# Half masks, transposes in two PSUM banks, and the output ahead of the state's sum, in a fused retention and MLP kernel

## Chip, cores, metric

One core of one Trainium2 chip. The metric is device time in microseconds (us), the median of a kernel's runs. PE is the tensor engine, DVE the vector engine, ACT the scalar engine, POOL GpSimd.

## The reference

Retention over q, k, v of shape (8, 8, 576, 64), followed by a dense layer, a Mish activation and a second dense layer. Cut to what matters:

```python
scores = (q @ k.T) / sqrt(64)
ret    = (scores * Dmat) @ v               # Dmat: gamma_h ** (i - j) for i >= j, else 0
x      = ret as 4608 tokens x 512
h      = x @ w_in                          # 512 x 2048
out    = (h * tanh(log1p(exp(h)))) @ w_out # 2048 x 512
```

## The kernel before

The sequence is cut into chunks of 128 positions; two chunks (same place, neighbouring batches) are a pair, four chunks a token block. For each chunk: P casts q and k to bf16 and scales them on DVE, T transposes them on PE and copies them out of PSUM, S makes the scores and masks them on DVE, O adds the product with v and the product with the running state of earlier chunks; the result, xT, feeds the dense layers. The state is summed per pair. Chunks 0 to 3 go through a start-up of their own with warming matmuls, chunks 4 to 7 are woven between blocks of the first dense layer, later ones go by pairs. Each engine gets its work in the order of the program text.

```python
def step_t(n):                       # transposes of chunk n, ACT and DVE copy them out
    tp = ps_sc.tile([P, 4, NP, P], BF16, name="sc")[:, 0:2]
    ...                              # PE: 4 transposes of q into tp[:, 0], 4 of k into tp[:, 1]
    for i, copy in enumerate((nc.scalar.copy, nc.vector.tensor_copy)):
        copy(r["qk"][:, i, u], tp[:, i])

def pair_o(m):                       # output of a pair
    sc = pairs[m][1][0]
    ot = sc.rearrange("p e (g u) i -> p e g u i", g=2)      # e: one PSUM bank each
    step_k(m)                        # PE: state products; DVE: their sum; cast to bf16
    ...                              # PE: within, across
    nc.vector.tensor_copy(xt[...], sc...)

# chunk 4 between the dense blocks i of token block 0
elif i == 8:  step_k(0)
elif i == 9:  step_n(1)              # DVE: two multiplications
elif i == 10: one(4, "P")
elif i == 12: one(4, "T")
elif i == 13: one(4, "S")
...
```

A PSUM tile of the pool `ps_sc` is 4 KB per partition. It is counted here as two banks: of its four parts (the first index of `tp`), 0 and 1 lie in one bank, 2 and 3 in the other. `[:, 0:2]` takes parts 0 and 1, `[:, ::2]` parts 0 and 2.

## Time and profile before

314.31 us (three runs).

| engine | busy us of 312.8 |
|---|---|
| PE | 300.0 |
| ACT | 136.0 |
| DVE | 123.4 |
| POOL | 78.6 |

PE is the bound. Here is pair 5's output, in order of time (start, length, engine, line, instruction, and in brackets the idle time before it and what ended it):

```profile
84.36 1.22 DVE L392 CAST xT<-sc 128x1024 bf16<-128x1024 f32 x1 [0.33 <-PE sc L361]
85.50 0.68 DVE L261 TENSOR_TENSOR qks<-qraw,gq 128x512 bf16<-128x512 f32 x1
85.64 1.90 PE L404 MATMUL hp<-xT,w_in_t 128*128 128x512 bf16 x8 [0.36 <-DVE xT L392]
```

PE stands 0.36 us for the copy that makes xT; DVE goes on with the next pair's casts at once.

### The profile page before, as it was taken

To read this page: it belongs to the slowest core of one execution; us is meant where nothing else is said; L and a number is where in the kernel's file an instruction comes from. 1 tells how busy PE (TensorE), PEld (TensorE's weight loads), DVE (VectorE), ACT (ScalarE), POOL (GpSimd) and SP (SyncE) were. 2 spreads that over 40 slices of the span, in tenths; PEclk is the share of its full clock that TensorE was granted. 3 is DMA by queue.
4 is the path that set the end of the run, shared out by engine and by line. 5 is a ranking of instruction groups with operands and counts; after the bars stand their busy time and mean duration, and the time that the engine had idled before them with its cause. 6 is when DMAs were issued, how large, how long until landed. Compare 5 with 4: busy or idle time off the path is not lost.

```text
span 312.8 us, 6059 instructions
## 1 busy us (share of the span) xinstructions
PE 300.0 (96%) x2601; PEld 157.2 (50%) x2637; DVE 123.4 (39%) x170; ACT 136.0 (43%) x237; POOL 78.6 (25%) x102
## 2 busy tenths in 40 slices
PE   6899989999999999999999999999999999999995
PEld 2355578655455545454545454545454544444444
DVE  3546465219768561626252526252525221000000
ACT  6665655422364633343434343434343433334311
POOL 6576573453340404040404040600000000000000
PEclk9999999999999999999999999999999999999999
DMA  6999999999998696959696959692313100000132
GB/s 180 255 186 226 198 207 226 201 232 248 214 230 103 132 174 141 168 137 169 142 165 143 160 144 159 138 160 63 90 47 88 48 34 36 34 34 36 40 81 80
DMA packets 71946, 43.38 MB, mean 139 GB/s; under 512 B 55664, under 2 KB 63088, under 8 KB 71920
## 3 DMA queue, kind: packets, MB, share of 16 engines
q0 software_dynamic: 43424, 26.22, 55.8%
q1 hardware_dynamic: 28352, 16.65, 20.6%
q8 instruction: 20, 0.33, 0.5%
q10 hardware_dynamic: 144, 0.13, 0.1%
q14 instruction: 6, 0.05, 0.0%
HBM read 36.70 MB, written 9.44 MB: 148 GB/s over the span
## 4 chain that ended last, share of the span: by engine, by line
PE 89%; ACT 4%; DVE 3%; issue 2%; DMA 1%; SPq 1%; ACTq 0%; DVEq 0%
PE hp L439 39%; PE hp L404 32%; PE hp L427 4%; PE sc L306 3%; PE sc L347 3%; ACT res L459 2%; PE sc L361 2%; DMA kraw<-in_k_dram 1%; PE sc L280 1%; PE hp L329 1%; PE hp L451 1%; DVE sm L309 1%; PE hp L415 1%; PE sc L329 1%; ACT qkT L282 1%
## 5 line engine op out<-in xcount | busy, mean ns | idle before, releaser
L439 PE MATMUL hp<-w_out_t,gT 128*128 128x512 bf16 x541 | 125.2, 379 | 1.2 <-issue 0.3
L404 PE MATMUL hp<-xT,w_in_t 128*128 128x512 bf16 x480 | 112.7, 379 | 1.3 <-DVE xT L392 0.4
L406 ACT ACTIVATE gT<-hp 128x512 bf16<-128x512 f32 x124 | 74.0, 597 | 36.6 <-PE hp L404 34.0
L439 PEld LDWEIGHTS <-gT 128*128 128x128 bf16 x560 | 53.3, 98 | 62.6
L404 PEld LDWEIGHTS <-w_in_t 128*128 128x128 bf16 x496 | 47.5, 97 | 57.1 <-DVE xT L392 0.9
L459 ACT COPY res<-hp 128x512 f32<-128x512 f32 x35 | 20.5, 585 | 98.4 <-PE hp L439 98.4
L309 DVE TENSOR_TENSOR sm<-sc,mask 128x1024 bf16<-128x1024 f32 x36 | 42.7, 1217 | 10.0 <-PE sc L306 10.0
L592 POOL COPY seen<-qkT 1x1 bf16<-1x1 bf16 x10 | 1.8, 176 | 121.9 <-DMA qkT<-qks 121.9
L336 DVE TENSOR_TENSOR st<-st,hp 128x512 f32<-128x512 f32 x8 | 5.5, 686 | 54.9 <-PE hp L329 54.9
L392 DVE CAST xT<-sc 128x1024 bf16<-128x1024 f32 x14 | 17.1, 1221 | 22.6 <-PE sc L361 22.2
L261 DVE TENSOR_TENSOR qks<-kraw,gk 128x512 bf16<-128x512 f32 x32 | 21.8, 683 | 1.7 <-DMA kraw<-in_k_dram 1.7
L261 DVE TENSOR_TENSOR qks<-qraw,gq 128x512 bf16<-128x512 f32 x32 | 21.8, 681 | 0.0
L112 POOL DMA_DIRECT2D qraw<-in_q_dram x16 | 17.2, 1075 | 13.9 <-DVE qks L261 9.1
L112 POOL DMA_DIRECT2D kraw<-in_k_dram x16 | 17.1, 1072 | 9.3 <-DVE ssb L338 3.7
L112 POOL DMA_DIRECT2D v<-in_v_dram x16 | 17.2, 1080 | 6.6 <-DMA kraw<-in_k_dram 2.5
L454 DVE COPY half<-hp 128x256 f32<-128x256 f32 x1 | 0.4, 425 | 43.8 <-PE hp L451 43.8
L427 PE MATMUL hp<-xT,w_in_t 128*128 128x128 bf16 x272 | 17.0, 219 | 0.0
L427 PEld LDWEIGHTS <-w_in_t 128*128 128x128 bf16 x272 | 15.5, 98 | 0.9 <-issue 0.2
L282 DVE COPY qkT<-sc 128x512 bf16<-128x512 bf16 x12 | 5.1, 422 | 23.4 <-ACT qkT L282 23.4
L429 ACT ACTIVATE gT<-hp 128x512 bf16<-128x512 f32 x17 | 10.1, 597 | 8.6 <-PE hp L427 8.6
L338 ACT CAST ssb<-st 128x512 bf16<-128x512 f32 x12 | 7.4, 618 | 14.3 <-DVE st L336 13.3
L306 PE MATMUL sc<-qkT 64*128 64x128 bf16 x288 | 11.9, 218 | 1.7 <-DVE qkT L282 1.5
(67 smaller groups left out, 163.6 us busy)
## 6 DMA issues: line engine op xcount, KB each, us to landing
out_dram<-res SPq DMA_DIRECT2D x31, 256.0 KB, 2.1
qraw<-in_q_dram POOLq DMA_DIRECT2D x12, 512.0 KB, 6.9
kraw<-in_k_dram POOLq DMA_DIRECT2D x12, 512.0 KB, 8.2
v<-in_v_dram POOLq DMA_DIRECT2D x12, 256.0 KB, 8.8
qraw<-in_q_dram POOLq DMA_DIRECT2D x8, 256.0 KB, 10.3
kraw<-in_k_dram POOLq DMA_DIRECT2D x8, 256.0 KB, 10.3
w_out_t<-in_moe_w_out_dram POOLq DMA_DIRECT2D x4, 512.0 KB, 11.7
qraw<-in_q_dram SPq DMA_DIRECT2D x8, 128.0 KB, 3.8
```

The costliest lines, as they stand in the source:

```text
L112: nc.gpsimd.dma_start(out=r[x][ds(off, ni)].rearrange("p u h d -> p (u h) d"), in_=src[ds(b, 2), :, ds(i0, ni), :].rearrange("b h p d -> p ...
L261: nc.vector.tensor_tensor(by_slots(r["qks"][:, i, u]), r[x][:, u].rearrange("p (r s) d -> p r s d", r=2), g[:, place(2 * m), :].rearrange( ...
L306: nc.tensor.matmul(sc[:, e, p, :], lhsT=qk[r, 1, u, p, :], rhs=qk[r, 0, u, p, :], start=True, stop=True)
L309: nc.vector.tensor_tensor(sm.rearrange("p e n i -> p (e n) i"), sc.rearrange("p e n i -> p (e n) i"), mask1.rearrange("p e n i -> p (e n) ...
L347: nc.tensor.matmul(ot[ds(64 * c, 64), e, g, :], lhsT=vs[:, h, :], rhs=sm[:, e, p, :], start=(start and g == 0), stop=True, skip_group_chec ...
L392: nc.vector.tensor_copy(xt[:, :, ds(s * P, 2 * P)].rearrange("p n (u i) -> p n u i", u=2), sc.rearrange("p e (g u) i -> p (e g) u i", g=2))
L404: nc.tensor.matmul(hp, lhsT=w_in_t[:, c, ts(f, P)], rhs=xts[t][:, c, :], start=(c == 0), stop=(c == KC - 1))
L406: nc.scalar.activation(gts[t][:, f, :], hp, AX.Mish)
L427: nc.tensor.matmul(hp[:, j, :], lhsT=w_in_t[:, c, ts(4 * fb + j, P)], rhs=xts[t][:, c, ts(s, P)], start=(c == 0), stop=(c == KC - 1))
L429: nc.scalar.activation(gts[t][:, ds(4 * fb, 4), ts(s, P)], hp, AX.Mish)
L439: nc.tensor.matmul(ops, lhsT=gts[t][:, f, ts(s, P)], rhs=w_out_t[:, f, :], start=(f == 0), stop=(f == nF - 1))
L459: copy(ot, ops)
```

## The change

Its intent is to shorten four waits of PE. The first two masks are done in halves, one per bank, with the next key cast between them. The two transposes of a chunk are put in two banks, so that ACT and DVE may copy at once. T and S of chunks 4 to 7 come one dense block earlier. In pair_o the output copy comes ahead of the state's sum, and for pair 5 it is shared by ACT and DVE. Cut to its core:

```diff
-        tp = ps_sc.tile([P, 4, NP, P], BF16, name="sc")[:, 0:2]
+        tp = ps_sc.tile([P, 4, NP, P], BF16, name="sc")[:, ::2]
 # step_s, chunks 0 and 1
+            for e in range(2):
+                nc.vector.tensor_tensor(sm[:, e], sc[:, e], mask1[:, e], op=OP.mult)
+                if e == 0:
+                    between()                 # the key cast of the next chunk
 # the state's cast to bf16
-        (nc.vector.tensor_copy if m < 4 else nc.scalar.copy)(ssb, st_sum[b])
+        (nc.vector.tensor_copy if b < 4 and i0 < 2 * P else nc.scalar.copy)(ssb, st_sum[b])
 # pair_o
-        step_k(m)
+        state = step_k(m)
 ...
+        if m == 5:
+            nc.scalar.copy(xv[:, 0], ot[:, 0])
+            nc.vector.tensor_copy(xv[:, 1], ot[:, 1])
+        else:
+            nc.vector.tensor_copy(...)
+        if state:
+            step_sum(*state)
 # chunk 4
         elif i == 9:
             step_n(1)
-        elif i == 10:
             one(4, "P")
-        elif i == 12:
+        elif i == 11:
             one(4, "T")
 # chunks 5 to 7: T at fb 0 (was 1), S at fb 1 (was 2), P ahead of the state
```

More of the change, by code (lines that the diff above doesn't have):

```diff
@@ L296, in step_n, with step_s @@
                 op=OP.mult)
-    def step_s(n):
+    def step_s(n, between=None):
         m, u = divmod(n, 2)
@@ L308, in step_s @@
         sm = tr.tile([P, 2, NP, P], BF16, name="sm")
-        nc.vector.tensor_tensor(
-            sm.rearrange("p e n i -> p (e n) i"), sc.rearrange("p e n i -> p (e n) i"),
-            mask1.rearrange("p e n i -> p (e n) i") if n < NCH else
-            (mask if len(chunks[n]) == 1 else mask2).unsqueeze(1).to_broadcast([P, 2 * NP, P]), op=OP.mult)
+        if between:
+            for e in range(2):
[3 more added lines that the diff above has]
+        else:
+            nc.vector.tensor_tensor(
+                sm.rearrange("p e n i -> p (e n) i"), sc.rearrange("p e n i -> p (e n) i"),
+                mask1.rearrange("p e n i -> p (e n) i") if n < NCH else
+                (mask if len(chunks[n]) == 1 else mask2).unsqueeze(1).to_broadcast([P, 2 * NP, P]), op=OP.mult)
         pairs[m][u] = (sc, sm)
@@ L317, in step_k @@
         if m >= n_pairs or len(chunks[2 * m]) > 1:
-            return
+            return None
         b, i0, _ = chunks[2 * m][0]
@@ L331, in step_k, with step_sum @@
                                      start=(u == 0 and p == 0), stop=True, skip_group_check=True)
+        return b, i0, st
+    def step_sum(b, i0, st):
         if i0 == 0:
@@ L391, in pair_o @@
         xt, s = x_of(2 * m)
-        nc.vector.tensor_copy(xt[:, :, ds(s * P, 2 * P)].rearrange("p n (u i) -> p n u i", u=2),
-                              sc.rearrange("p e (g u) i -> p (e g) u i", g=2))
+        xv = xt[:, :, ds(s * P, 2 * P)].rearrange("p (e g) (u i) -> p e g u i", e=2, u=2)
+        if m == 5:
+            nc.scalar.copy(xv[:, 0], ot[:, 0])
+            nc.vector.tensor_copy(xv[:, 1], ot[:, 1])
+        else:
+            nc.vector.tensor_copy(xv.rearrange("p e g u i -> p (e g) u i"), ot.rearrange("p e g u i -> p (e g) u i"))
+        if state:
+            step_sum(*state)
     gts = {}
@@ L487 @@
     keep_warm(3)
-    first(0, "VS")
-    first(1, "Qk")
+    first(0, "V")
+    step_s(0, lambda: first(1, "k"))
+    first(1, "Q")
     keep_warm(3)
@@ L499 @@
     keep_warm(3)
-    first(1, "S")
-    first(2, "Qk")
+    step_s(1, lambda: first(2, "k"))
+    first(2, "Q")
     keep_warm(3)
@@ L536 @@
         elif i == 8:
-            step_k(0)
+            step_sum(*step_k(0))
         elif i == 9:
             step_n(1)
-        elif i == 10:
             one(4, "P")
-        elif i == 12:
+        elif i == 11:
             one(4, "T")
@@ L555 @@
             if n < 7:
-                if fb == 1:
+                if fb == 0:
                     one(n + 1, "T")
-                elif fb == 2:
+                elif fb == 1:
                     one(n + 1, "S")
-                    if n % 2 == 0:
-                        step_k(n // 2)
                     if n < 6:
                         one(n + 2, "P")
+                    if n % 2 == 0:
+                        step_sum(*step_k(n // 2))
                 elif fb == 3:
@@ L578, in visit @@
             if m == 5:
-                step_k(1)
+                step_sum(*step_k(1))
             one(n, "T")
```

## The prediction

> **What bounds the kernel now.** I read the page's shares first, then the waits of the tensor engine (PE) by window, then the order of time in the two windows where those waits lie, then the landing times of the loads.
>
> ```profile
> PE 300.0 (96%) x2601; PEld 157.2 (50%) x2637; DVE 123.4 (39%) x170; ACT 136.0 (43%) x237; POOL 78.6 (25%) x102
> ```
>
> PE is busy for 300.0 of 312.8 us, so a change that touches no matmul can only take idle PE time, about 12.8 us. Of that, some 3.5 us lie behind the last matmul (305.80 + 3.51 = 309.3 in the chain of work that ended last, against a span of 312.8), and the change leaves the tail alone. What is left I get from the waits of PE in the first 100 us; from 125 us on the same view lists none.
>
> ```profile
> PE hp L244 <- DVE qks L234: 2.8, 3, 1.4
> PE sc L306 <- DVE qkT L282: 1.5, 4, 0.6
> PE sc L172 <- DVE idle L162: 1.3, 1, 1.3
> PE hp L404 <- DVE xT L392: 0.4, 1, 0.4
> PE hp L415 <- ACT xT L380: 0.3, 1, 0.3
> PE sc L347 <- DVE sm L309: 0.3, 1, 0.3
> ```
>
> Columns: waiter, what it waited for, us in total, times, longest. The first row is the start-up: transposes of the first chunks behind the vector engine's (DVE) casts. The second is the scores of chunks 4 to 7 behind the copies of their transposes. The fourth is the first matmul of token block 2 behind pair 5's output copy, at 85.64 us. The change aims at exactly these rows. Start-up work is also padded with idle warming matmuls (L172, 9.2 us busy), so there "busy" is not work: what counts is when the first dense matmuls are fed.
>
> **What the Trainium skill says.** "PSUM — Partial Sum Buffer", section "PSUM bank collisions raise a hardware error": two engines must not touch one bank and quadrant at once, reads against reads included, so the two are kept apart by a dependency. The trace agrees. In the old step_t both transposes lie in one bank, and DVE's copy starts only as the scalar engine's (ACT) ends:
>
> ```profile
> 31.59 0.58 ACT L282 COPY qkT<-sc 128x512 bf16<-128x512 bf16 x1
> ...
> 32.20 0.42 DVE L282 COPY qkT<-sc 128x512 bf16<-128x512 bf16 x1 [1.21 <-ACT qkT L282]
> ...
> 32.68 0.40 PE L306 MATMUL sc<-qkT 64*128 64x128 bf16 x8 [0.31 <-DVE qkT L282]
> ```
>
> ACT ends at 32.17, DVE starts at 32.20, PE stands 0.31. The same page, section "Engine vs sequencer instructions", says that the queues of ACT and DVE are strict FIFO: an instruction that waits holds all behind it. Rival 2 and the pair-5 item rest on that. The trace has it: the cast of key chunk 1 starts at 10.10 behind the 1.22 us mask of 8.96, though its load was issued at 5.41 and landed 4.1 us later (its tile's view), at 9.5.
>
> **The change part by part.**
>
> (a) Masks in halves, chunks 0 and 1. A half, 128x512 from PSUM, costs an estimated 0.68 (the 128x512 fp32 sums of L336 take 686 ns on average), the next instruction following 0.6 after its start. Chunk 0: mask half 8.96 to 9.57, then the cast at about 9.57 in place of 10.10: the turn of key 1 comes 0.5 earlier. Chunk 1: key 2 was issued at 8.0 and landed 4.9 later, at 12.9; its cast goes from 13.59 to about 12.92, 0.65 earlier. The other half is done a little later than the undivided mask in this case, but PE comes to it later too. Carried through scores, mask 2 and output 2, whose lengths stay, the first dense matmul (L415, 18.07) starts at about 17.4: **0.65 gained at the start**.
>
> It is not kept. The dense blocks run on weights that come in order of column. The load for blocks 4 to 7 is the second of these two issues:
>
> ```profile
> L127 POOL DMA_DIRECT2D w_in_t<-in_moe_w_in_dram x2: 747/806/864, 13.4 to 14.3; - x2
> ...
> DMA to landing us min/median/max: 4.9/6.6/8.3
> ```
>
> 14.3 + 8.3 = 22.6. And PE comes to block 4 at just that time:
>
> ```profile
> 21.68 1.05 PE L427 MATMUL hp<-xT,w_in_t 128*128 128x128 bf16 x16
> 22.61 1.68 PE L404 MATMUL hp<-xT,w_in_t 128*128 128x512 bf16 x6
> ```
>
> The change moves no load and the queues are full there (DMA digits 9 from the second slice on), so the landing stays. A PE that is 0.65 early waits about 0.6 at block 4. Part (a) is worth 0.05 us.
>
> (b) Transposes in two banks, chunks 4 to 7, with T and S moved one block earlier. The serial part removed is DVE's 0.42 plus a hand-over, some 0.5. Chunk 5: wait of 0.28 gone. Chunk 6: wait of 0.60 falls to about 0.15, as ACT's copy itself starts late there (44.08, behind a Mish activation, ending 44.67; PE is free for the scores at 44.58). Chunk 6's output, which waited 0.32 for its mask, now has two blocks (2 x 0.95) between scores and output against 0.45 + 1.22 of score and mask: 0.32 gone. Chunk 7: 0.28 gone. Chunk 4: 0.31 gone. Sum: 0.28 + 0.45 + 0.32 + 0.28 + 0.31 = **1.64 gained**.
>
> (c) Chunk 4's transposes one block earlier (step 11 in place of 12). Its cast was moved up in the text too, but not in DVE's queue, where it stays behind step_n(1):
>
> ```profile
> 28.51 1.29 DVE L293 TENSOR_TENSOR ks<-sc,gk 128x512 bf16<-128x512 bf16 x2 [0.26 <-PE sc L290]
> 29.71 0.68 DVE L261 TENSOR_TENSOR qks<-qraw,gq 128x512 bf16<-128x512 f32 x1
> 30.31 0.68 DVE L261 TENSOR_TENSOR qks<-kraw,gk 128x512 bf16<-128x512 f32 x1
> ...
> 28.31 2.75 PE L404 MATMUL hp<-xT,w_in_t 128*128 128x512 bf16 x11
> 30.90 0.61 PE L280 MATMUL sc<-ident,qks 128*128 128x128 bf16 x8
> ```
>
> The casts end at 30.39 and 30.99. PE came to the transposes at 30.90, in time. One block (four matmuls, 0.87) earlier is 30.04: 0.39 of waiting for the query cast, then, four transposes later (4 x 0.055), at 30.67, 0.36 for the key cast. **0.75 lost.**
>
> (d) Output ahead of the state's sum, pair 5's copy split. The copy of 128x1024 (1.22, from 84.36) becomes 128x512 on each engine, in separate banks (the split is over e, and e is the bank): ready at about 85.05, PE free at 85.28, so the wait of 0.36 goes. But sum and state cast (0.68 + 0.43) now run after it on DVE, and pair 6's casts start at 86.1, not 85.50. Their first key cast ends at about 87.4; PE, now 0.36 earlier, wants it at 87.25: 0.15 back. **0.2 gained.** In other pairs PE waits for neither, so the order is worth nothing.
>
> (e) The state cast of pair 3 moves from DVE to ACT (condition on b and i0 in place of m < 4). In chunk 6's stretch it now stands in ACT's queue ahead of the Mish of block 1, while it waits for DVE's mask (1.22) and sum (0.68). Counted from the scores' start: sum done at 2.3, cast 2.9, Mish 3.45; PE wants that block's PSUM buffer (the pool hp has two) for block 3 at about 3.2. **0.3 lost.**
>
> Sum: 0.05 + 1.64 - 0.75 + 0.2 - 0.3 = 0.84 us. 314.31 - 0.84 = 313.5. I lean a little further, to **313.3**, since (c) and (e) are chains of estimates on PE arrival times whose losses shrink if PE arrives later than I think, while the gains of (b) are waits that the trace records.
>
> **The rivals.**
>
> 1. The start-up gain is kept. For it: the half masks do free casts whose data had landed, and 2.8 us of waits stand there. Against it: the landing at 22.6 under full queues. If the weights happened to land earlier, the 0.65 would stay: about 312.7.
>
> 2. ACT or DVE becomes the bound in chunks 4 to 7, through the FIFO: transposes or scores one block early find their casts, copies or PSUM buffers not ready. For it: (c) and (e). Against it: each engine is busy for only 5 to 6 of 10 us there in the table of windows. If it costs twice what I say, 314.4, no gain at all.
>
> 3. All waits listed go and nothing comes back: 0.65 + 1.64 + 0.36 = 2.65, so 311.7. I hold this for the optimistic bound; it is still under 1%.
>
> 4. A held PSUM buffer in the later pairs: from pair 6 on the state sits in the pool hp, and its sum now follows the output copy by some 1.2 us. The next use of that buffer is 3.5 us later (16 matmuls of L439 between), so it should be hidden; if not, up to ten pairs would each lose some tenths and the kernel would be slower, about 315.5.
>
> **Range and chances.** Rivals 1 and 2 bracket most of it, 312.7 to 314.4; the three runs of before spread by 0.9, and rival 3 has some weight: 312.0 to 314.4. Two per cent is 6.3 us, more than all the idle PE time in reach (12.8 less the tail of 3.5 less the first 1.3 is 8.0, most of it small or bound to loads). So within 2%: 0.98; faster 0.01; slower 0.01.
>
> **What would show it.** (a) right: L415 starts near 17.4 and PE then waits about 0.6 for w_in at block 4, with the load landing again at 22.6; wrong: no such wait. (b) right: the row of L306 behind qkT falls from 1.5 to under 0.3, and ACT and DVE copies of L282 overlap. (c) right: L280 waits for DVE's L261, about 0.75 near 30 us. (d) right: no wait of L404 behind xT at 85 us, perhaps a small one of L280 near 87. (e) right: near 51 us a block of L427 waits for an ACT Mish of L429. The steady part after 125 us should show no PE wait. The prediction falls if the weights land at another time, or if a wait from rival 4 appears in every pair.

## The result, and the profile after

The changed kernel takes 315.11 us (314.98 to 315.24, four runs), the kernel before 314.46 us in the same rounds. The ratio is 1.002, with a 95% interval of 1.0003 to 1.0038. Ratios here are formed from the fast runs of the same rounds, so not quite the ratios of the medians. It is within 2%, as predicted, but on the slow side, and outside the stated range of 312.0 to 314.4: the sum gave 0.84 us of gain (1.0 with the lean to 313.3), and about 0.65 was lost.

PE's waits in the changed kernel, with the same columns as before:

```profile
PE hp L244 <- DVE qks L234: 2.7, 3, 1.3
PE sc L172 <- DVE idle L162: 1.3, 1, 1.3
PE sc L280 <- DVE qks L261: 0.9, 4, 0.3
PE sc L306 <- DVE qkT L282: 0.9, 3, 0.3
PE sc L358 <- DVE sm L312: 0.4, 2, 0.2
PE hp L445 <- ACT gT L447: 0.2, 1, 0.2
```

Three of chunks 5 to 7's waits for qkT are still there, at 0.3 us each. Four waits of transposes (L280) behind DVE's casts are new, and so is one for ACT. The wait for xT is gone from the list, but not what it cost, as will be seen.

**Where the time went.** A list of waits does not add up to a time. I therefore cut the run at five points that can be read from the order of time: the first 128x512 matmul on w_in (block 4), chunk 4's scores, the first matmul on w_out, the scores of pair 6, and the end of the last matmul. Each column is the length of one stretch in us, the difference of two such times:

| kernel | start to block 4 | to chunk 4's scores | to first w_out | to pair 6's scores | to last matmul |
|---|---|---|---|---|---|
| before | 22.61 | 10.07 | 25.16 | 33.12 | 218.34 |
| changed | 22.93 | 10.51 | 24.77 | 33.51 | 218.31 |
| difference | +0.32 | +0.44 | -0.39 | +0.39 | -0.03 |

The differences sum to 0.73 us; the spans differ by 0.7 (312.8 and 313.5). In the twelve profiles of the experiments the last four stretches repeat to about 0.03 us wherever the code of the stretch is the same, with one exception told below. Only the first varies from run to run. So one profile is enough to judge an edit behind block 4, although the total time scatters by half a microsecond.

### The profile page after: what moved, and what is told of

It reads as the page before. It is cut to its first block, busy times and chain, and to the rows that moved or that the text cites. A ratio compares the mean times of both kernels' runs of the same rounds, so it can differ in the third digit from the quotient of the medians.

```text
span 313.5 us, 6088 instructions
## 1 busy us (share of the span) xinstructions
PE 303.2 (97%) x2637; PEld 157.3 (50%) x2637; DVE 122.7 (39%) x172; ACT 136.5 (44%) x238; POOL 78.6 (25%) x102
## 4 chain that ended last, share of the span: by engine, by line
PE 89%; DVE 4%; ACT 2%; DMA 2%; SPq 1%; issue 1%; DVEq 0%
PE hp L457 39%; PE hp L422 33%; PE hp L445 4%; PE sc L306 3%; PE sc L358 3%; PE sc L372 2%; DMA kraw<-in_k_dram 2%; SPq L142 1%; PE sc L280 1%; PE hp L336 1%; PE hp L469 1%; DVE qks L261 1%; PE hp L433 1%; PE sc L336 1%; DVE qks L234 1%
## 5 line engine op out<-in xcount | busy, mean ns | idle before, releaser
L457 PE MATMUL hp<-w_out_t,gT 128*128 128x512 bf16 x560 | 126.7, 379 | 0.0
L422 PE MATMUL hp<-xT,w_in_t 128*128 128x512 bf16 x496 | 114.0, 379 | 0.0
L409 DVE CAST xT<-sc 128x1024 bf16<-128x1024 f32 x13 | 15.9, 1225 | 96.5 <-PE sc L372 78.2
L316 DVE TENSOR_TENSOR sm<-sc,mask 128x1024 bf16<-128x1024 f32 x34 | 40.3, 1219 | 7.9 <-PE sc L306 7.9
L358 PE MATMUL sc<-sm,v 128*64 128x128 bf16 x288 | 12.0, 221 | 0.6 <-DVE sm L312 0.4
```

The lines of the kernel that those rows point to most:

```text
L316: nc.vector.tensor_tensor(sm.rearrange("p e n i -> p (e n) i"), sc.rearrange("p e n i -> p (e n) i"), mask1.rearrange("p e n i -> p (e n) ...
L358: nc.tensor.matmul(ot[ds(64 * c, 64), e, g, :], lhsT=vs[:, h, :], rhs=sm[:, e, p, :], start=(start and g == 0), stop=True, skip_group_chec ...
L409: nc.vector.tensor_copy(xv.rearrange("p e g u i -> p (e g) u i"), ot.rearrange("p e g u i -> p (e g) u i"))
L422: nc.tensor.matmul(hp, lhsT=w_in_t[:, c, ts(f, P)], rhs=xts[t][:, c, :], start=(c == 0), stop=(c == KC - 1))
L457: nc.tensor.matmul(ops, lhsT=gts[t][:, f, ts(s, P)], rhs=w_out_t[:, f, :], start=(f == 0), stop=(f == nF - 1))
```

## The experiments

The theory after this reading: three stretches are each the work of one part of the change. Chunk 4's transposes came a block earlier, and their casts did not (+0.44). The copies still do not overlap, so chunks 5 to 7 gained only what the earlier place of T and S brings, and pair 5's shared copy is longer than the whole one (+0.39). The start (+0.32) is taken for chance. The rivals: the steady part got slower, the halves cost time, or the bank or the shared destination is what keeps the copies apart. Every run gave correct results.

| run | rounds | median us | before us | ratio (95%) | stretches: block 4; scores 4; w_out; pair 6; last |
|---|---|---|---|---|---|
| undo_t4 | 5 | 314.74 | 314.66 | 0.9998 (0.9986, 1.0010) | 22.93; 10.06; 24.77; 33.51; 218.33 |
| undo_pair5 | 5 | 314.60 | 314.66 | 0.9999 (0.9986, 1.0012) | 22.44; 10.49; 24.77; 33.12; 218.34 |
| undo_masks | 5 | 314.94 | 314.66 | 1.0016 (1.0001, 1.0032) | 23.76; 10.50; 24.79; 33.51; 218.34 |
| two_tiles | 5 | 314.68 | 314.66 | 1.0000 (0.9982, 1.0019) | 23.38; 10.49; 23.70; 33.51; 218.33 |
| after_again | 5 | 314.97 | 314.64 | 1.0024 (0.9994, 1.0054) | 25.89; 10.48; 24.77; 33.51; 218.33 |
| masks_only | 5 | 314.87 | 314.64 | 0.9999 (0.9986, 1.0011) | 23.18; 10.07; 25.41; 33.12; 218.33 |
| best | 5 | 311.81 | 314.64 | 0.9910 (0.9897, 0.9922) | 22.63; 9.69; 23.37; 32.73; 218.34 |
| best_nomask | 5 | 311.88 | 314.64 | 0.9914 (0.9898, 0.9930) | 22.79; 9.70; 23.36; 32.73; 218.34 |
| one_bank | 0 | 315.15 | 314.52 | single | 22.87; 10.50; 24.77; 33.51; 218.34 |
| t4_cast_first | 0 | 313.98 | 314.52 | single | 22.52; 9.68; 24.77; 33.52; 218.34 |
| pair5_halves | 0 | 313.89 | 314.52 | single | 22.38; 10.49; 24.77; 32.74; 218.33 |
| state3_dve | 0 | 314.44 | 314.52 | single | 22.50; 10.50; 24.43; 33.52; 218.33 |

The last four are single runs of unknown state; only their stretches behind block 4 are used.

**1. Chunk 4 back in its place.**

```diff
             step_n(1)
-            one(4, "P")
-        elif i == 11:
+        elif i == 10:
+            one(4, "P")
+        elif i == 12:
             one(4, "T")
```

> The changed kernel, with chunk 4's cast and transposes back at steps 10 and 12. Theory: in the changed kernel PE stands twice (0.28 and 0.20 us) at chunk 4's transposes behind DVE's casts, and the first output block is 0.4 us further behind there than at step 4; so this run should be 0.3 to 0.5 us faster than the changed kernel (about 314.7), and the waits of L280 near 30 us should be gone. Rival (the loss lies in the steady part or in the start): no change, 315.1.

The second stretch falls from 10.51 to 10.06, the value of the kernel before; the others stay. The median is 0.4 us under that of the first runs of the changed kernel, but those were other rounds, so I rest on the stretch. The part costs 0.44 us. In the changed kernel the two halves of the transposes stand one after the other:

```profile
30.78 0.40 PE L280 MATMUL sc<-ident,qks 128*128 128x128 bf16 x4 [0.28 <-DVE qks L261]
31.38 0.40 PE L280 MATMUL sc<-ident,qks 128*128 128x128 bf16 x4 [0.20 <-DVE qks L261]
```

**2. Chunk 4 early, with its cast really early.**

```diff
-            step_n(1)
             one(4, "P")
+            step_n(1)
         elif i == 11:
             one(4, "T")
```

> The changed kernel with chunk 4's cast ahead of step_n(1) in DVE's queue. Theory: the stretch from block 4 to chunk 4's scores falls from 10.5 to 9.7 us (the kernel before has 10.07), the waits of L280 near 30 us gone; stretches behind it as in the changed kernel. Rival (key chunk 4's load is too late for it): 10.1 or more, with a wait of DVE's L261 for the load.

9.68 us: 0.83 less than the changed kernel and 0.39 less than the kernel before. The early transposes were right; their producer was left behind the two multiplications of step_n in DVE's queue. The rival, a load that comes too late, is refuted.

**3. Two tiles in place of two banks.**

```diff
-        tp = ps_sc.tile([P, 4, NP, P], BF16, name="sc")[:, ::2]
+        tp = [ps_sc.tile([P, 4, NP, P], BF16, name="sc")[:, 0] for i in range(2)]   # n < 8
```

> The changed kernel, with the two transposes of chunks 4 to 7 in two separately allocated PSUM tiles in place of two banks of one tile. Theory: the copies are serial because the tile as a whole orders its readers, not the bank, so here DVE's copies of L286 in chunks 4 to 7 start without waiting for ACT's and the scores' waits (3 x 0.3 us) go: 0.6 to 0.9 us faster than the changed kernel, about 314.4. Rival (the order comes from the bank or from the shared SBUF tile that both write): DVE still waits for ACT, time as the changed kernel's.

In the changed kernel, chunk 5's copies, from two banks of one tile, are serial:

```profile
37.75 0.58 ACT L282 COPY qkT<-sc 128x512 bf16<-128x512 bf16 x1
...
38.36 0.43 DVE L282 COPY qkT<-sc 128x512 bf16<-128x512 bf16 x1 [1.99 <-ACT qkT L282]
```

With two tiles DVE starts even ahead of ACT, which still has an activation to finish:

```profile
38.13 0.42 DVE L286 COPY qkT<-sc 128x512 bf16<-128x512 bf16 x1 [1.33 <-PE sc L284]
38.18 0.58 ACT L286 COPY qkT<-sc 128x512 bf16<-128x512 bf16 x1
```

The third stretch falls from 24.77 to 23.70, and no wait for qkT is left on PE. Both copies still write the same SBUF tile, so the shared destination was not what ordered them. The total did not show the full 1.07 us, a miss of the expected 314.4: in the profiled run PE waited 0.8 us for w_in near the start (block 4 at 23.38), and the six runs scatter from 313.53 to 315.57.

**4. Back to one bank.**

```diff
-        tp = ps_sc.tile([P, 4, NP, P], BF16, name="sc")[:, ::2]
+        tp = ps_sc.tile([P, 4, NP, P], BF16, name="sc")[:, 0:2]
```

> The changed kernel with both transposes back in the first bank of their tile. Theory: the second bank changed nothing, since the tile's readers are kept in order whatever their bank: DVE's copy still starts as ACT's ends, and the stretch from chunk 4's scores to the first output matmul stays 24.77 us (to 0.05). Rival (the banks gave some overlap): that stretch is longer by 0.3 us or more. Single time about 315, not used.

24.77, as in the changed kernel, and DVE's copy again starts as ACT's ends (38.26):

```profile
37.68 0.58 ACT L282 COPY qkT<-sc 128x512 bf16<-128x512 bf16 x1
...
38.29 0.42 DVE L282 COPY qkT<-sc 128x512 bf16<-128x512 bf16 x1 [1.99 <-ACT qkT L282]
```

The second bank changed nothing. With run 3 this settles it: what orders the two readers in this program is the tile, not the bank.

**5. Pair 5 and the sum undone.**

```diff
         state = step_k(m)
+        if state:
+            step_sum(*state)
 ...
-        if m == 5:
-            nc.scalar.copy(xv[:, 0], ot[:, 0])
-            nc.vector.tensor_copy(xv[:, 1], ot[:, 1])
-        ...
+        nc.vector.tensor_copy(...)             # whole, in every pair; pair 5's state cast on ACT
```

> The changed kernel, with the state's sum ahead of the output again in all pairs, pair 5's copy whole on DVE and its state cast on ACT. Theory: the split copy is serial (ACT, then DVE) and the sum behind it delays pair 6's casts, which cost PE 0.21 + 0.20 us of waits at 87.75 and 88.35; so 0.3 to 0.4 us faster than the changed kernel (about 314.7), the waits of L280 near 88 us gone and that of L422 behind xT (0.4) back. Rival (order of sum and output gained time and the loss is elsewhere): slower than the changed kernel.

The fourth stretch falls from 33.51 to 33.12, the value of before, so this part cost 0.39 us: order, shared copy and the place of the state cast together, which no run separates. The last stretch does not move: the new order of sum and output is worth nothing in pairs 6 and later. What happened in the changed kernel, in order of time:

```profile
84.73 0.58 ACT L406 CAST xT<-sc 128x512 bf16<-128x512 f32 x1 [4.01 <-PE sc L372]
85.34 0.69 DVE L407 CAST xT<-sc 128x512 bf16<-128x512 f32 x1 [1.71 <-ACT xT L406]
85.48 2.06 PE L422 MATMUL hp<-xT,w_in_t 128*128 128x512 bf16 x8
...
85.95 0.68 DVE L347 TENSOR_TENSOR st<-st,sc 128x512 f32<-128x512 f32 x1
86.67 0.43 DVE L349 CAST ssb<-st 128x512 bf16<-128x512 f32 x1
87.01 0.69 DVE L261 TENSOR_TENSOR qks<-qraw,gq 128x512 bf16<-128x512 f32 x1
87.61 0.68 DVE L261 TENSOR_TENSOR qks<-kraw,gk 128x512 bf16<-128x512 f32 x1
87.75 0.40 PE L280 MATMUL sc<-ident,qks 128*128 128x128 bf16 x4 [0.21 <-DVE qks L261]
88.35 0.40 PE L280 MATMUL sc<-ident,qks 128*128 128x128 bf16 x4 [0.20 <-DVE qks L261]
```

DVE's half waits for ACT's, so xT is whole at 86.03, 1.30 us after the copy began, where one DVE copy takes 1.22. Then come the sum and the state cast, and pair 6's casts start at 87.01. In the kernel before they started at 85.50. PE waits for them twice. A wait hides inside another row as well: the eight matmuls from 85.48 on take 2.06 us where the kernel before needs 1.90.

**6. Pair 5 in two halves on one engine.**

```diff
-            nc.scalar.copy(xv[:, 0], ot[:, 0])
+            nc.vector.tensor_copy(xv[:, 0], ot[:, 0])
             nc.vector.tensor_copy(xv[:, 1], ot[:, 1])
 # and the sum ahead of the output again, pair 5's state cast on ACT
```

> The changed kernel with the sum ahead of the output and pair 5's copy as two halves on DVE. Theory: the first matmul of the next token block needs only the first half, so the stretch from the first output matmul to pair 6's scores is 32.75 us, against 33.5 in the changed kernel and 33.12 in the kernel before. Rival (the first matmul waits for all of xT): 33.1.

32.74, which is 0.77 under the changed kernel and 0.38 under the kernel before. In order of time:

```profile
84.17 0.69 DVE L408 CAST xT<-sc 128x512 bf16<-128x512 f32 x1 [0.33 <-PE sc L372]
84.77 0.68 DVE L409 CAST xT<-sc 128x512 bf16<-128x512 f32 x1
84.92 2.04 PE L422 MATMUL hp<-xT,w_in_t 128*128 128x512 bf16 x8
```

PE starts as the first half is done (84.86). The first two matmuls of a block read only the first half of xT, so two copies in a row on one engine hide most of the second behind them; not all, as the eight matmuls take 2.04 us against 1.90 in the kernel before. This is the gain that the shared copy was meant to bring.

**7. Pair 3's state cast back on DVE.**

```diff
-nc.vector.tensor_copy if b < 4 and i0 < 2 * P else ...
+nc.vector.tensor_copy if b < 4 and i0 < 2 * P or b == 0 and i0 == 2 * P else ...
```

> The changed kernel with the state cast of pair 3 back on DVE. Theory: the wait of 0.21 us of PE behind ACT's Mish near 53.7 us goes, and the stretch from chunk 4's scores to the first output matmul falls from 24.77 to 24.55. Rival: unchanged.

The wait is gone and the stretch is 24.43, so the move to ACT cost 0.34 us, more than the 0.21 that the list of waits shows.

**8. Whole masks again, the halves alone, and the changed kernel once more.** In undo_masks the first masks are whole, in masks_only the halves are the only change to the kernel before, and after_again is the changed kernel unaltered.

```diff
-    first(0, "V")                             # undo_masks, and the same for chunk 1
-    step_s(0, lambda: first(1, "k"))
-    first(1, "Q")
+    first(0, "VS")
+    first(1, "Qk")
```

> The changed kernel, with whole masks in chunks 0 and 1. Theory: the first dense blocks are paced by the landing of the weights and the first loads, which differ from run to run by some tenths, so the masks are worth nothing: within 0.2 us of the changed kernel, block 4 starting at 22.6 to 22.9. Rival: the halves are worth what the prediction worked out at the start (0.65 us at the first dense matmul), so this run is about 0.6 us slower than the changed kernel; or they cost 0.3 us, as the first profile has it, and this run is 0.3 faster.

> The kernel before with the halved first masks alone. Theory: the halves gain up to 0.5 us only where key chunk 1 lands while the first mask runs; where it lands behind the mask the second half comes later than the whole would have, and costs 0.2 to 0.3 us. Landing is chance, so within 0.3 us of the kernel before (314.4 to 315.0), all stages behind block 4 as in the kernel before (10.07, 25.16, 33.12, 218.3). Rival (the gain of the prediction is kept): 0.5 us faster, 314.1.

> The changed kernel once more, unaltered, for a second set of times and a second profile of its start. Theory: the stages behind the start repeat to within 0.05 us (block 4 to chunk 4's scores 10.5, from there to the first output matmul 24.8, from there to pair 6's scores 33.5, from there to the end 218.3), a net loss of 0.4 us against the kernel before; the start differs with the landing of the loads. So 314.9 to 315.3. Rival (the loss in the first profile was chance): 314.4 or less.

after_again repeats the four late stretches to 0.03 us. Its total loss, about 0.3 us by the medians, is smaller than the first 0.65; the interval is wide because of one run of 318.12 us, told of in the last section. The halves could not be told from chance. With halves, block 4 starts between 22.38 and 25.89 us in eleven profiles, median 22.87; with whole masks at 22.61, 22.79 and 23.76. masks_only against before: ratio 0.9999 (a gain of 0.5 us would be 0.9984, just outside its interval). Nor does any profile with halves have the early first dense matmul (see part (a) below). So the rival of a kept 0.5 us is refuted, and any cost is under the noise. undo_masks missed its expected window of 22.6 to 22.9 with 23.76: PE waited 1.1 us there for a load of w_in.

masks_only also missed one expectation behind block 4: 25.41 us in place of 25.16. The row that differs is a state cast on DVE, 1.02 us long in this run against 0.51 in the kernel before. The casts behind it are 0.5 us later, and PE loses 0.26 at chunk 6's transposes. The last point of the last section has what goes with its length.

**9. All faults mended.** Runs 2, 3, 6 and 7 together (pair 5's state cast on ACT, pair 3's on DVE), with half masks (best) and with whole ones (best_nomask).

> The changed kernel with each fault mended: chunk 4's cast ahead of step_n(1) in DVE's queue; two separate PSUM tiles for the transposes of chunks 4 to 7; the sum ahead of the output again, with pair 5's copy in two halves that both run on DVE; the state cast of pair 3 on DVE. Theory: block 4 to chunk 4's scores 9.75, then 23.5, then 32.75, so 1.5 to 2.5 us faster than the kernel before behind the start: 312.3 to 313.2. Rival (waits come back elsewhere): no faster than the kernel before.

> The same as the run named best, with whole first masks as in the kernel before. Theory: same time as that run within 0.3 us, the halves being worth nothing on average. Rival: 0.5 us slower (the halves gain what the prediction said) or 0.3 us faster (they cost).

311.81 and 311.88 us, 0.9% under the kernel before and clear of noise. The stretches are 9.69, 23.37 and 32.73, the sum of what the single edits gained. Both are faster than either kernel, and below the 312.3 to 313.2 that was expected of best: the four late stretches alone are 2.56 us shorter than in the kernel before (284.13 against 286.69). PE's waits in best, all of them:

```profile
PE hp L244 <- DVE qks L234: 2.1, 3, 1.1
PE sc L172 <- DVE idle L162: 1.3, 1, 1.3
PE sc L362 <- DVE sm L316: 0.4, 2, 0.2
PE hp L437 <- ACT xT L395: 0.3, 1, 0.3
PE hp L426 <- DMA w_in_t<-in_moe_w_in_dram: 0.2, 1, 0.2
```

All of them lie in the start-up; behind block 4 the list has no wait.

## Why the prediction was wrong

**Part (a), halves: that they are worth nothing came true, but by luck, as the way to it was wrong.** It said that the first dense matmul comes 0.65 us earlier and that the landing of w_in then eats the gain. The landing stayed indeed (22.5 in the changed kernel's profile, 22.6 before), but the first dense matmul came at 18.27, not at 17.4, and PE did not wait for w_in. In the eleven profiles with halves it comes at 17.77 to 18.52, median 17.99; with whole masks at 18.00, 18.07 and 18.28. Two steps failed. One took the landing of key chunk 1 from one profile as fixed. In the changed kernel's profile the load came after the first half was done:

```profile
8.56 0.69 DVE L312 TENSOR_TENSOR sm<-sc,mask 128x512 bf16<-128x512 f32 x1 [0.79 <-PE sc L306]
10.28 0.43 DVE L234 TENSOR_SCALAR qks<-kraw 128x512 bf16<-128x512 f32 x1 [1.03 <-DMA kraw<-in_k_dram]
10.62 0.69 DVE L312 TENSOR_TENSOR sm<-sc,mask 128x512 bf16<-128x512 f32 x1
```

A whole mask from 8.56 on would have been done before 10.28, so here the cut freed nothing. Over all profiles that key lands between 9.4 and 10.2 us. The other step is the clause that the second half is done later "but PE comes to it later too". The outputs of chunks 0 and 1 wait for that half, 0.2 us each (the row of L358 above), in all eleven profiles with halves, also where the key came early (two_tiles, cast at 9.52), and in none of the three with whole masks. What was right is the limit by the landing: in best PE reaches block 4 early and waits there for the load that lands at 22.6 (the last row of its list).

The start's 0.32 is not explained in full. 0.20 of it stands at the first dense matmul and 0.12 behind it. In four profiles, the changed kernel's among them, the cast of key chunk 3 takes 0.9 us in place of 0.42, and the way from the first dense matmul to block 4 is 4.66 to 4.67 us. It is 4.49 to 4.50 in the three profiles with halves, a short cast and no wait for a load (one_bank, t4_cast_first, pair5_halves). No run tests this, and how much of the rest is chance stays open.

**Part (b), two banks: this is the step that failed.** The prediction put "Chunk 5: wait of 0.28 gone", the same for 7 and most of 6's wait, on the skill's rule of banks ("PSUM — Partial Sum Buffer", section "PSUM bank collisions raise a hardware error"): two engines are kept apart if they touch one bank, so two banks set them free. The trace of the kernel before agreed with the rule, but it could not tell a bank from a tile, since both copies lay in one bank of one tile. Here the program orders the readers of a tile, and DVE waits for ACT from two banks just as from one (runs 3 and 4). Of the 1.33 us that part (b) promised for chunks 5 to 7, the stretch shows 0.39 net. Adding back the 0.34 of part (e) makes 0.73, which is left to the earlier place of T and S, since run 4 leaves nothing to the banks: chunk 6's wait for its mask (0.32) is gone and its wait for qkT (0.60) halved; the last 0.11 is not placed. Two tiles bring 1.07 more. Chunk 4's wait of 0.31 went as promised, but by luck: not by the banks (one_bank has it gone too), but because its T came a block earlier and its S did not.

**Part (c) was right.** It gave 0.75 us of new waiting, against the 0.31 of old that (b) counts for chunk 4: a net loss of 0.44. Measured: 0.44. The list of waits has only 0.28 + 0.20 of it. It counts from the modelled ends of matmuls: the two sets of transposes start 0.60 us apart where four in a row take 0.22, so PE stood 0.38 at the second set, and 0.20 is listed; the last 0.09 is not placed.

**Part (d) failed on the same step.** The copy "ready at about 85.05" supposed that the copies run at once. They are serial, and in place of 0.2 gained there is 0.39 lost. That the delayed casts of pair 6 would cost PE something was foreseen, but mis-sized: they started at 87.01, not at 86.1. Of these 0.9 us, 0.37 is that the whole place comes later here (the copy begins at 84.73, not at 84.36), and the rest is about the 0.61 that DVE's half stood behind ACT's. That the order is worth nothing in other pairs was right: the last stretch is 218.3 us in all profiles.

**Part (e) was right**: 0.3 predicted, 0.34 measured.

**The sum.** Without (a), and with (b) at 0.73 for chunks 5 to 7 and 0.31 for chunk 4, and (d) at -0.39, the sum 1.04 - 0.75 - 0.39 - 0.34 is -0.44: the loss of the three middle stretches (0.44 - 0.39 + 0.39). The rest of the loss is the start's, and is open. So one false premise, used twice, turned a small gain into a small loss. The lean to 313.3 made it worse: it rested on "the gains of (b) are waits that the trace records". A recorded wait is only a gain if the edit removes its cause. Of the rivals, number 4 did not appear (no PE wait after 125 us), and number 2 named the right place: its reason, work held up in an engine's queue, held for (c) and (e), but not for the copies. Number 1 did not come true, nor number 3; its 311.7 is near the 311.81 of best, which has edits that the change lacked.

## What to carry to other kernels

Before counting on two engines running at once, change only the thing that is to set them free and look in the trace whether the wait between them goes. Here readers were ordered by tile, so two tiles helped and a second bank inside one tile did nothing. Where a consumer is moved earlier, follow its producer in its engine's queue and move that too, and where a consumer reads its input in parts, two copies in a row on one engine can hide more than a shared copy. Cut the run at fixed points and compare stretches: they repeat to a few hundredths of a microsecond where totals scatter by half of one.

## What the Trainium skill lacked or had wrong

- "PSUM — Partial Sum Buffer", section "PSUM bank collisions raise a hardware error", gives bank and quadrant as what must be kept apart. It does not say that a kernel's own dependencies may be coarser. Here two banks of one tile were ordered (DVE's copy at 38.36, as ACT's ended at 38.33), while two tiles overlapped (38.13 and 38.18) with correct results.
- "TensorE: Matmul & The Clock Gate", section "HAM oscillation — how this bites in real kernels", gives the rule of no PE gaps over about 3.4 us. In the profiled run of after_again a wait of 1.77 us for w_in was followed by a granted clock of 0.50 from 22 to 25 us, and that run took 318.12 us against 314.56 to 315.48 for its other five. A wait of 1.1 us in undo_masks left the clock at 1.00. It is one case, and makes no new rule. The rows of after_again (window, its length, PE busy, and so on; the clock is third from the end):

```profile
20.00:21.00 1.00, 0.00 (x0) 0.00 (x0) 0.39 (x1) 0.41 (x1) 0.12 (x1) 1.00 1.27 198
21.00:22.00 1.00, 0.34 (x2) 0.23 (x3) 0.00 (x0) 0.00 (x0) 0.10 (x1) 0.88 1.27 209
22.00:23.00 1.00, 1.00 (x6) 0.21 (x4) 0.00 (x0) 0.00 (x0) 0.80 (x1) 0.50 1.20 269
```

- No page has the spread of landing times. The second load of w_in, issued between 12.9 and 14.0 us, landed between 18.0 and 21.6 us over fourteen profiles, and PE waited for it in three of them, 0.8 to 1.8 us; in two more PE waited for the first or the third load, 0.6 and 0.2 us.
- "SBUF — State Buffer", section "Who interferes with whom", has the port that DVE and GpSimd share. The record shows a pattern in both directions: now DVE's instruction is the longer, now GpSimd's. Near 17 us GpSimd issues a load of k and DVE casts key chunk 3 (L234, 128x512). Where the cast begins 0.26 to 0.28 us after the issue (the changed kernel, undo_t4, undo_pair5, state3_dve), it takes 0.89 to 0.90 us. In the other ten profiles it takes 0.41 to 0.42; in three of them it begins 0.19 to 0.20 after the issue (before, undo_masks, best_nomask), and there the issue takes 1.09 to 1.10 us in place of 0.92 to 0.93. The state cast near 42 us varies likewise: in ten profiles it begins 0.38 to 0.89 us after an issue and takes 1.02 to 0.52 us, so that it always ends 1.40 to 1.42 us after the issue began. The 1.02 us of masks_only are one of these. That fits the page, but no run here moves the issue to test it.
